# Filter rows by part in natural column order, in a spectral-mixing and MLP kernel on one core

## The chip, the cores and the metric

The kernel runs on one core of a Trainium2 chip. The metric is the device time of one execution in microseconds (us), median of several executions. A run's state is called fast when it is undisturbed; all timed comparisons below use fast runs. The engines are named as in the profile: PE is TensorE's matmul, PEld its weight load, DVE is VectorE, ACT is ScalarE, POOL is GpSimd, SP is SyncE, which issues most DMA transfers. TensorE's results go to PSUM, in this kernel in banks of 512 fp32 per partition; the other operands lie in SBUF, and an "eviction" is the copy from PSUM to SBUF. The "stationary" operand of a matmul is the one that the weight load brings in. The "tail" is what follows the last computed output.

## The reference

A sequence of 2048 positions with 512 features goes through two residual blocks. The first multiplies its two-dimensional real Fourier transform by a complex filter; the second is an MLP over the sequence axis.

```python
def _A_ref(x, w_r, w_i):                 # x: 1 x 2048 x 512, w: 2048 x 257
    X = jnp.fft.rfft2(x.astype(jnp.float32), axes=(-2, -1))
    X = X * (w_r + 1j * w_i)
    return jnp.fft.irfft2(X, s=(S, D), axes=(-2, -1)).astype(jnp.bfloat16)

h  = x + _A_ref(_layernorm(x), A_w_r, A_w_i)
h2 = h + _B_ref(_layernorm(h), B_w1, B_b1, B_w2, B_b2)   # MLP over S, 1376 hidden, gelu
```

## The kernel before

All transforms are matrix products. The parts that matter here:

- "Transform 2" turns Y into half spectra along the features. Even and odd columns of the spectrum need different sums, so it has two parities `par`. Its eviction goes to CS.
- "Mixing" (X) combines the rows of CS in two half-height matmuls, so that each of 128 partitions holds a component of one row. Partition order is given by `_row`.
- The "filter multiply" V = PSUM x W on VectorE multiplies the mixed values by the real and by the imaginary part of the filter (index `w` or "part").
- "G1" uses slices of V as the stationary operand of the first inverse step.

CS and V are kept parity by parity: first the 128 odd columns, then the 128 even ones. The filter lies in memory in natural column order, so VectorE reads it with a step of two.

```python
def _row(sign, comp, k2, s):
    return 4 * (k2 * 2 + s) + 2 * sign + comp
...
add("CS", [NP, 16, 2, 2, NP], bf, rd)     # group, parity, component, column
add("W", [NP, NG, 2, LW], bf, rw)         # filter: row group, part, 257 columns
add("V", [NP, NG, 2, 256], bf, rv)
...
# filter loads: rows of 514 bytes, 28 transfers in all
for comp in range(2):
    d = W[comp::4, g0:g0 + ng, w, :]
    dma(..., d, bass.AP(dram.tensor, g0 * LW, [[64 * LW, 32], [LW, ng], [1, LW]]), ...)
    d = W[2 + comp::4, h0:h0 + nh, w, :]  # mirrored rows, in descending order
    dma(..., d, bass.AP(dram.tensor, (64 - h0) * LW, [[64 * LW, 32], [-LW, nh], [1, LW]]), ...)
...
# transform 2: four matmuls fill one PSUM bank of 512 fp32, then one eviction
mm(f"f2_{G}_{par}{b}", lambda bank, par=par: ps[:, bank, par * 256:par * 256 + 256],
   Y[:, b, par, 2 * G:2 * G + 2, :]..., E[:, b, par, :], unit, b == 0, b == 1, ...)
dst = CS[:, G, :, :, :].rearrange("p y c j -> p (y c j)")
cs_ops[G] = act(f"cs_{G}", dst, lambda bank: ps[:, bank, :], ACT.Copy, 512, unit=unit, prio=14)
...
# mixing, then the filter multiply on VectorE
mm(f"x_{G}_{c}{r}", ..., M[rows, ..., c, :], CS[rows, G, :, c, :], ...)
win = bass.AP(wt.tensor, wt.offset + 1, [list(wt.ap[0]), [LW, 2 * ng], [1, 2], [2, NP]])
eng.tensor_tensor(vout, s, win, ALU.mult)   # s: fp32 in PSUM, each row used for both parts
...
# G1
mm(f"g1_{g}_{par}{w}", ..., V[:, g, w, par * NP:par * NP + NP], R[:, 1 if g == 0 else 0, w, :], ...)
```

A list scheduler in the kernel fixes the order of each engine's instructions when the program is built.

Of the kernel before, what the change touches and what calls it, by code (L numbers as in the profile page):

```python
# [9 lines left out]
NP = 128  # L10
# [3 lines left out]
NG = 32  # L14
F_LEN = 1376
NFT = 11
LW = 257
# [17 lines left out]


def _row(sign, comp, k2, s):
    return 4 * (k2 * 2 + s) + 2 * sign + comp


def _fwd_matrices(special):
# [381 lines left out]
def memory_layout():  # L423
    L = []
    bf = dt.bfloat16
    f32 = dt.float32
    cur = [0]

    def region(nbytes):
        o = cur[0]  # L430
        cur[0] += (nbytes + 31) // 32 * 32
        return o

    def add(name, shape, dty, off):
        L.append((name, shape, dty, off))
        return off

    add("X", [NP, NS2, D_LEN], bf, region(16384))
    rb = region(16384)
    add("PQ", [NP, 2, 2, NS2, NP], bf, rb)  # L440
    add("GT", [NP, NFT, D_LEN], bf, rb)
    rc = region(16384)
    add("Y", [NP, 2, 2, NG, 64], bf, rc)
    add("EO", [NP, NS2, D_LEN], bf, rc)
    add("OUT", [NP, NS2, D_LEN], bf, rc)
    rd = region(16384)
    add("CS", [NP, 16, 2, 2, NP], bf, rd)
    add("H", [NP, NS2, D_LEN], bf, rd)
    rw = region(2 * NG * LW * 2)
    add("W", [NP, NG, 2, LW], bf, rw)  # L450
    add("HH", [NP, NS2, D_LEN], bf, rw)
    rv = region(32768)
    add("V", [NP, NG, 2, 256], bf, rv)
    add("W1", [NP, NS2, F_LEN], bf, region(NS2 * F_LEN * 2))
    for t in range(NFT):
        add(f"W2_{t}", [NP, S_LEN], bf, rv + t * 4096 if t < 8 else rw + 16384 + (t - 8) * 4096)
    add("FP", [NP, NS2, 2, NP], bf, region(8192))
    add("FS", [NP, NS2, 2, NP], bf, rv)
    add("EM", [NP, 3072], bf, region(6144))
    add("IF", [NP, NS2, NP], bf, region(4096))  # L460
    for i in range(3):
        add(f"TT{i}", [NP, 2, 256], f32, region(2048))
    for i in range(4):
        add(f"JK{i}", [NP, D_LEN], bf, region(1024))
    add("st", [NP, NS2, 8], f32, region(512))
    add("mv", [NP, NS2, 2], f32, region(128))
    for nm in ("sm", "nm", "v1", "rs", "v2", "r2"):
        add(nm, [NP, NS2], f32, region(64))
    add("eps", [NP, 8], f32, region(32))
    add("ZT", [NP, D_LEN], bf, region(1024))  # L470
    add("bv", [NP, NS2], f32, region(64))
    add("tb", [NP, 8], f32, region(32))
    add("B1s", [NP, 16], bf, region(32))
    add("B1f", [NP, 16], f32, region(64))
    add("B2s", [NP, NS2], bf, region(32))
    add("B2f", [NP, NS2], f32, region(64))
    return L
# [13 lines left out]
def build_kernel(nc, A_x, A_w_r, A_w_i, B_w1, B_b1, B_w2, B_b2, out):  # L491
# [29 lines left out]
    def mm(name, outf, lhsT, rhs, unit, start, stop, first, prio, n, ins=None, half=False, after=()):  # L521
        occ = n / 2.4 + 3.0
        if half:
            occ = occ / 2
        if n == 128:
            occ = 61.0
        return K.op(name, "pe", lambda eng, bank: eng.matmul(outf(bank), lhsT, rhs, start=start, stop=stop),  # L527
                    ins=ins or [lhsT, rhs], occ=occ, lat=n / 2.4 + 220.0, unit=unit, pw=True, first=first, prio=prio, after=after)
# [46 lines left out]
    for ch, (u0, u1) in enumerate(((0, 1), (1, 4), (4, 8))):  # L575
        g0, ng = 4 * u0, 4 * (u1 - u0)
        lst = []
        for w, dram in ((0, A_w_r), (1, A_w_i)):
            for comp in range(2):
                d = W[comp::4, g0:g0 + ng, w, :]  # L580
                lst.append(dma(f"ld_wp{ch}_{w}{comp}", d, bass.AP(dram.tensor, g0 * LW, [[64 * LW, 32], [LW, ng], [1, LW]]),
                               32 * ng * 514, prio=42 - ch, group=f"w{ch}", rate=300.0))
                h0, nh = (g0, ng) if g0 else (1, ng - 1)
                d = W[2 + comp::4, h0:h0 + nh, w, :]
                lst.append(dma(f"ld_wm{ch}_{w}{comp}", d, bass.AP(dram.tensor, (64 - h0) * LW, [[64 * LW, 32], [-LW, nh], [1, LW]]),
                               32 * nh * 514, prio=42 - ch, group=f"w{ch}", rate=300.0))
                if g0 == 0:
                    d = W[2 + comp::4, 0, w, :]
                    lst.append(dma(f"ld_wz{ch}_{w}{comp}", d, bass.AP(dram.tensor, 32 * LW, [[64 * LW, 32], [1, LW]]),
                                   32 * 514, prio=42 - ch, group=f"w{ch}", rate=300.0))  # L590
        for u in range(u0, u1):
            wload[u] = lst
    dma("ld_D2", EM[:, 2048:3072], cin["EM"][:, 2048:3072], 1 << 18, outs=[EM[:, 2048:3072]], prio=30)
# [72 lines left out]
    for q in range(8):  # L666
        for b in range(2):
            unit = PsumUnit("f1", 1)
# [28 lines left out]
    def stage_f2(u):  # L697
        for i in range(2):
            G = 2 * u + i
            unit = PsumUnit("f2", 1)  # L700
            for par in range(2):
                for b in range(2):
                    mm(f"f2_{G}_{par}{b}", lambda bank, par=par: ps[:, bank, par * 256:par * 256 + 256],
                       Y[:, b, par, 2 * G:2 * G + 2, :].rearrange("p g k -> p (g k)"), E[:, b, par, :],
                       unit, b == 0, b == 1, par == 0 and b == 0, 10, 256)
            dst = CS[:, G, :, :, :].rearrange("p y c j -> p (y c j)")
            if G == 1:
                cs_ops[G] = dve(f"cs_{G}", lambda eng, bank, dst=dst: eng.tensor_copy(dst, ps[:, bank, :]), [], [dst], 512, unit=unit, prio=14)
            else:
                cs_ops[G] = act(f"cs_{G}", dst, lambda bank: ps[:, bank, :], ACT.Copy, 512, unit=unit, prio=14)  # L710

    def stage_x(u):
        unit = PsumUnit("x", 2)
        first = True
        grp = [cs_ops[2 * u + 1]]
        for i in range(2):
            G = 2 * u + i
            for c in range(2):
                for r in range(2):
                    rows = slice(64 * r, 64 * r + 64)  # L720
                    mm(f"x_{G}_{c}{r}", lambda bank, r=r, i=i: ps[:, bank + r, i * 256:i * 256 + 256],
                       M[rows, 1 if G == 0 and r == 0 else 0, c, :], CS[rows, G, :, c, :], unit, c == 0, c == 1, first, 13, 256, half=True, after=grp)
                    first, grp = False, ()
        g0 = 4 * u
        nh = 2 if u in V_SPLIT else 1
        ng = 4 // nh
        for h in range(nh):
            wt = W[:, g0 + h * ng:g0 + h * ng + ng, :, :]
            win = bass.AP(wt.tensor, wt.offset + 1, [list(wt.ap[0]), [LW, 2 * ng], [1, 2], [2, NP]])
            vout = V[:, g0 + h * ng:g0 + h * ng + ng, :, :].rearrange("p g w l -> p (g w l)")  # L730

            def tt(eng, bank, h=h, win=win, vout=vout):
                s = psf[:, bank * 512 + h * 512:bank * 512 + h * 512 + 256 * ng]
                s = bass.AP(s.tensor, s.offset, [list(s.ap[0]), [256, ng], [0, 2], [1, 256]])
                return eng.tensor_tensor(vout, s, win, ALU.mult)  # L735
            K.op(f"v_{u}_{h}", "dve", tt, ins=[wt], outs=[vout], occ=50.0 + 2130.0 / nh, lat=170.0 + 2130.0 / nh, unit=unit, pr=True,
                 last=h == nh - 1, prio=11, after=wload[u])
# [3 lines left out]
    def stage_g1(u):  # L741
        for h in range(2):
            nw = G1_WARM.get((u, h), 0)
            unit = PsumUnit("g1", 1, early=nw > 0)
            for w_ in range(nw):
                warm(f"warmg{u}{h}{w_}", unit, 10, first=w_ == 0, after=[lastg1[0]])
            for gi in range(2):
                g = 4 * u + 2 * h + gi
                for par in range(2):
                    for w in range(2):  # L750
                        lastg1[0] = mm(f"g1_{g}_{par}{w}", lambda bank, gi=gi, par=par: ps[:, bank, gi * 256 + par * 128:gi * 256 + par * 128 + 128],
                           V[:, g, w, par * NP:par * NP + NP], R[:, 1 if g == 0 else 0, w, :], unit, w == 0, w == 1,
                           gi == 0 and par == 0 and w == 0 and not nw, 12, 128)
            g0 = 4 * u + 2 * h
            dst = PQ[:, :, :, :, 4 * g0:4 * g0 + 8].rearrange("p y q n (g k) -> p (y q n) g k", k=4)

            def src(bank):
                return ps[:, bank, :].rearrange("p (g m k) -> p m g k", g=2, k=4)
            act(f"pq_{u}_{h}", dst, src, ACT.Copy, 512, unit=unit, prio=15)
# [117 lines left out]
```

## Time and profile before

| What | Before |
|---|---|
| time, median of 3 runs | 134.35 us (134.19 to 134.53) |
| span of the profiled execution | 133.0 us |
| first V multiply starts, last one ends | 22.0, 39.9 us |
| V multiplies | 17.9 us, no gap |
| spacing of transform-2 matmuls | 0.109 us |

The chain of waits goes back from the last instruction to what released it. Columns: start in us, length in us, what.

```profile
17.63 1.47 ACT Y L545 x3
...
19.15 2.77 PE ps L527 x25
...
22.02 1.04 DVE V L735
...
23.16 15.62 DVE V L735 x8
...
38.91 0.62 PE ps L527 x8
```

So from 22 to 39.9 us VectorE decides, and TensorE matters only if it makes VectorE wait. The groups by shape tell what one instruction of this part costs. Columns: line, engine, operation, output and inputs, shapes, count; busy time and mean ns of one; idle time before, with what ended it.

```profile
L527 PEld LDWEIGHTS ps<-GT,W 128*128 128x128 bf16 x160 | 23.1, 144 | 11.5
...
L735 DVE TENSOR_TENSOR V<-ps,W 128x2048 bf16<-128x2048 f32 x6 | 13.3, 2282 | 0.0
...
L527 PE MATMUL ps<-EM,Y 128*128 128x256 bf16 x64 | 8.7, 273 | 0.4 <-ACT Y L545 0.4
...
L527 PEld LDWEIGHTS ps<-EM,V 128*128 128x128 bf16 x128 | 7.5, 98 | 2.3 <-issue 1.4 <-DVE V L735 0.8
```

The mean of a matmul (273 ns in transform 2) is its latency; what it takes from TensorE is the spacing of starts (0.109 us), which the timeline shows (start, length of the whole group, operation, count):

```profile
25.21 1.91 PE L527 MATMUL ps<-EM,Y 128*128 128x256 bf16 x16
27.06 0.61 PE L527 MATMUL ps<-CS,EM 64*128 64x256 bf16 x8
27.60 0.45 PE L527 MATMUL ps<-EM,V 128*128 128x128 bf16 x5
```

Within the first group the spacing is (1.91 - 0.273) / 15 = 0.109 us.

The windows view gives busy times in a stretch (PE, PEld, DVE, ACT, POOL), then granted clock, DMA share and GB/s. While the filter arrives (16 to 30 us) the DMA engines are full at 280 GB/s; with the MLP's first weights, in rows of 11 KB (40 to 45 us), they reach 428.

```profile
16.00:30.00 14.00, 13.48 (x155) 9.91 (x153) 11.66 (x14) 10.70 (x23) 1.81 (x8) 1.00 1.03 280
40.00:45.00 5.00, 4.31 (x40) 3.47 (x40) 1.83 (x5) 3.61 (x8) 0.00 (x0) 1.00 1.02 428
```

### The profile page before, as it was taken

To read this page: it belongs to the slowest core of one execution; us is meant where nothing else is said; L and a number is where in the kernel's file an instruction comes from. 1 tells how busy PE (TensorE), PEld (TensorE's weight loads), DVE (VectorE), ACT (ScalarE), POOL (GpSimd) and SP (SyncE) were. 2 spreads that over 40 slices of the span, in tenths; PEclk is the share of its full clock that TensorE was granted. 3 is DMA by queue.
4 is the path that set the end of the run, shared out by engine and by line. 5 is a ranking of instruction groups with operands and counts; after the bars stand their busy time and mean duration, and the time that the engine had idled before them with its cause. 6 is when DMAs were issued, how large, how long until landed. Compare 5 with 4: busy or idle time off the path is not lost.

```text
span 133.0 us, 2023 instructions
## 1 busy us (share of the span) xinstructions
PE 125.4 (94%) x786; PEld 75.3 (57%) x786; DVE 69.2 (52%) x127; ACT 63.4 (48%) x146; POOL 12.2 (9%) x33
## 2 busy tenths in 40 slices
PE   6999989999987979999999999999999999999990
PEld 2356756878656726644434444456666666666660
DVE  0379975999990999999970000000242332423322
ACT  4569976878966999986679322222000000000000
POOL 0288830000300000000000000000000000000000
PEclk9999999999999999999999999999999999999999
DMA  3999698999999999992000000000111112111121
GB/s 94 335 370 382 178 276 229 304 317 264 411 430 430 398 411 409 419 281 89 0 0 0 0 0 0 5 0 0 39 39 64 55 39 81 42 59 59 39 79 39
DMA packets 16648, 22.16 MB, mean 167 GB/s; under 512 B 2720, under 2 KB 12960, under 8 KB 16128
## 3 DMA queue, kind: packets, MB, share of 16 engines
q1 hardware_dynamic: 16352, 21.52, 47.3%
q10 hardware_dynamic: 288, 0.52, 1.3%
q8 instruction: 6, 0.10, 0.3%
q14 instruction: 2, 0.02, 0.0%
HBM read 19.95 MB, written 2.10 MB: 166 GB/s over the span
## 4 chain that ended last, share of the span: by engine, by line
PE 51%; DVE 33%; ACT 8%; DMA 5%; issue 1%; SPq 1%; DVEq 0%; ACTq 0%
PE ps L527 50%; DVE V L735 13%; DVE H L795 7%; DMA X<-in_A_x_dram 5%; ACT Y L545 5%; DVE TT L786 4%; DVE TT L788 4%; DVE HH L800 4%; ACT rs L545 1%; ACT FS L545 1%; DVE st L649 1%; SPq L517 1%; DVE OUT L825 1%; ACT PQ L545 0%; PE ps L617 0%
## 5 line engine op out<-in xcount | busy, mean ns | idle before, releaser
L527 PE MATMUL ps<-HH,W 128*128 128x512 bf16 (+1 forms) x176 | 40.7, 379 | 1.2 <-DVE HH L800 0.9
L527 PE MATMUL ps<-GT,W 128*128 128x512 bf16 (+1 forms) x176 | 38.2, 379 | 0.0
L825 DVE SCALAR_TENSOR_TENSOR OUT<-ps,B2f,H 128x512 bf16<-128x512 f32 x16 | 12.0, 750 | 48.7 <-PE ps L527 48.7
L527 PEld LDWEIGHTS ps<-GT,W 128*128 128x128 bf16 (+1 forms) x176 | 25.4, 144 | 12.7
L527 PEld LDWEIGHTS ps<-HH,W 128*128 128x128 bf16 (+1 forms) x176 | 17.2, 100 | 21.2 <-DVE HH L800 1.9
L735 DVE TENSOR_TENSOR V<-ps,W 128x2048 bf16<-128x2048 f32 (+1 forms) x10 | 17.9, 1856 | 0.9 <-PE ps L527 0.9
L545 ACT ACTIVATE GT<-ps,B1f 128x512 bf16<-128x512 f32 (+1 forms) x11 | 7.1, 688 | 14.6 <-PE ps L527 14.6
L545 ACT ACTIVATE JK<-H,nm 128x512 bf16<-128x512 bf16 x16 | 11.6, 724 | 3.0 <-DVE H L795 2.9
L617 PE MATMUL ps<-ZT 128*128 128x512 bf16 x34 | 11.3, 479 | 1.3 <-DVE ZT L613 1.2
L649 DVE BATCH_NORM_STATS2 st<-X 128x6 f32<-128x512 bf16 x14 | 9.3, 668 | 5.3 <-DMA X<-in_A_x_dram 5.3
L795 DVE TENSOR_TENSOR H<-ps,TT 128x512 bf16<-128x512 f32 x16 | 10.9, 681 | 0.0
L545 ACT ACTIVATE PQ<-ps 128x512 bf16<-128x512 f32 x16 | 8.9, 603 | 3.5 <-PE ps L527 3.2
L545 ACT ACTIVATE EO<-ps 128x512 bf16<-128x512 f32 x16 | 9.3, 599 | 0.9 <-PE ps L527 0.9
L527 PE MATMUL ps<-EM,V 128*128 128x128 bf16 x128 | 9.2, 219 | 0.5 <-DVE V L735 0.5
L527 PE MATMUL ps<-EM,PQ 128*128 128x256 bf16 x64 | 9.0, 273 | 0.7 <-ACT PQ L545 0.7
L545 ACT ACTIVATE CS<-ps 128x512 bf16<-128x512 f32 x15 | 8.3, 608 | 2.1 <-PE ps L527 2.1
L527 PE MATMUL ps<-EM,Y 128*128 128x256 bf16 x64 | 8.7, 273 | 0.4 <-ACT Y L545 0.4
L527 PEld LDWEIGHTS ps<-EM,V 128*128 128x128 bf16 x128 | 7.5, 98 | 2.3 <-issue 1.4
L629 POOL TENSOR_SCALAR FS<-FP,rs 128x256 bf16<-128x256 bf16 x9 | 8.3, 935 | 1.3 <-ACT rs L545 1.3
L527 PE MATMUL ps<-FS,X 128*128 128x256 bf16 x64 | 8.3, 273 | 0.1
L786 DVE TENSOR_TENSOR TT<-ps,X 128x256 f32<-128x256 f32 x16 | 6.7, 416 | 3.3 <-PE ps L527 3.3
L527 PEld LDWEIGHTS ps<-EM,PQ 128*128 128x128 bf16 x64 | 6.2, 98 | 2.9 <-ACT PQ L545 0.9
(36 smaller groups left out, 80.3 us busy)
## 6 DMA issues: line engine op xcount, KB each, us to landing
W<-in_B_w_dram SPq DMA_DIRECT2D x4, 1376.0 KB, 11.0
W<-in_B_w_dram SPq DMA_DIRECT2D x10, 512.0 KB, 17.6
out_dram<-OUT SPq DMA_DIRECT2D x16, 128.0 KB, 1.7
W<-in_A_w_r_dram SPq DMA_DIRECT2D x4, 257.0 KB, 4.3
W<-in_A_w_i_dram SPq DMA_DIRECT2D x4, 257.0 KB, 5.0
X<-in_A_x_dram SPq DMA_DIRECT2D x4, 256.0 KB, 5.8
X<-in_A_x_dram SPq DMA_DIRECT2D x2, 512.0 KB, 7.7
W<-in_A_w_r_dram SPq DMA_DIRECT2D x4, 192.8 KB, 3.5
```

What stands on the lines that cost most here:

```text
L517: return eng.dma_start(dst, src)
L527: return K.op(name, "pe", lambda eng, bank: eng.matmul(outf(bank), lhsT, rhs, start=start, stop=stop), ins=ins or [lhsT, rhs], occ=occ, la ...
L545: return eng.activation(dst, s, func, **kw)
L617: return K.op(name, "pe", lambda eng, bank: eng.matmul(ps[:, bank, :], ZT[:, 0:NP], ZT[:, :], start=True, stop=True), ins=[ZT[:, :]], occ= ...
L629: dve(f"fs{i}", lambda eng, bank: eng.tensor_scalar(FS[:, i, :, :], FP[:, i, :, :], rs, None, op0=ALU.mult), [FP[:, i, :, :], rs], [FS[:, ...
L649: dve(f"st_{i}", lambda eng, bank, i=i, x=x: eng.bn_stats(ST[:, i, 0:6], x), [x], [ST[:, i, 0:6]], 512, prio=25)
L735: return eng.tensor_tensor(vout, s, win, ALU.mult)
L786: dve(f"tl_{s2}", lambda eng, bank, tt=tt, xl=xl: eng.tensor_tensor(tt[:, 0, :], ps[:, bank, 256:512], xl, ALU.add), [xl], [tt[:, 0, :]], ...
L788: dve(f"th_{s2}", lambda eng, bank, tt=tt, xh=xh: eng.tensor_tensor(tt[:, 1, :], xh, ps[:, bank, 256:512], ALU.subtract), [xh], [tt[:, 1, ...
L795: return eng.tensor_tensor(hs.rearrange("p (h d) -> p h d", h=2), e, tt[:, :, :], ALU.add)
L800: dve(f"hh_{s2}", lambda eng, bank, s2=s2, hs=hs: eng.tensor_scalar(HH[:, s2, :], hs, NM[:, s2:s2 + 1], R2[:, s2:s2 + 1], op0=ALU.add, op1 ...
L825: dve(f"fin{s2}", lambda eng, bank, dst=dst, bia=bia, hs=hs: eng.scalar_tensor_tensor(dst, ps[:, bank, :], bia, hs, op0=ALU.add, op1=ALU.add),
```

## The change

The filter is kept part by part (real, then imaginary), rows next to each other. With a new partition order, the un-mirrored rows of both components come in one transfer whose rows are as long as the chunk (2 to 8 KB), and 28 filter transfers become 20. VectorE then reads the filter contiguously, in natural column order. CS and V must be in that order too. TensorE makes it: transform 2 writes each parity into every second fp32 of the PSUM bank, and G1 picks a parity by loading every second column of V.

```diff
-    return 4 * (k2 * 2 + s) + 2 * sign + comp
+    return 4 * (k2 * 2 + s) + 2 * comp + sign
...
-    add("CS", [NP, 16, 2, 2, NP], bf, rd)
+    add("CS", [NP, 16, 2, 256], bf, rd)
-    add("W", [NP, NG, 2, LW], bf, rw)
+    add("W", [NP, 2, NG, LW], bf, rw)
...
+            d = W[0:NP:2, w, g0:g0 + ng, :].rearrange("p g l -> p (g l)")
+            lst.append(dma(f"ld_wp{ch}_{w}", d, bass.AP(dram.tensor, g0 * LW, [[64 * LW, 32], [0, 2], [1, ng * LW]]), ...))
             for comp in range(2):
-                d = W[comp::4, g0:g0 + ng, w, :]
-                lst.append(dma(f"ld_wp{ch}_{w}{comp}", d, bass.AP(dram.tensor, g0 * LW, [[64 * LW, 32], [LW, ng], [1, LW]]), ...))
-                d = W[2 + comp::4, h0:h0 + nh, w, :]
+                d = W[1 + 2 * comp::4, w, h0:h0 + nh, :]
...
-                    mm(f"f2_{G}_{par}{b}", lambda bank, par=par: ps[:, bank, par * 256:par * 256 + 256],
+                    mm(f"f2_{G}_{par}{b}", lambda bank, par=par: ps[:, bank, :].rearrange("p (c j y) -> p y c j", c=2, y=2)[:, par, :, :],
...
-                       M[rows, 1 if G == 0 and r == 0 else 0, c, :], CS[rows, G, :, c, :], ...
+                       M[rows, 1 if G == 0 and r == 0 else 0, c, :], CS[rows, G, c, :], ...
...
-            win = bass.AP(wt.tensor, wt.offset + 1, [list(wt.ap[0]), [LW, 2 * ng], [1, 2], [2, NP]])
+            win = bass.AP(wt.tensor, wt.offset + 1, [list(wt.ap[0]), [LW, ng], [NG * LW, 2], [1, 256]])
...
-                           V[:, g, w, par * NP:par * NP + NP], R[:, 1 if g == 0 else 0, w, :], ...
+                           V[:, g, w, par::2], R[:, 1 if g == 0 else 0, w, :], ...
```

## The prediction

> **What bounds the kernel now.** The chain of waits (133.0 us profile) has four parts. Until 19.1 us: loads of x, statistics and forward transform 1 (ACT's Y evictions at the end). Then transform 2 ("F2", matmuls ps<-EM,Y) and the first mixing matmuls ("X", ps<-CS,EM) up to 22.0. From 22.0 to about 39.9 VectorE multiplies by the filter (V<-ps,W): ten instructions without a gap, 17.9 us. After that VectorE again (43 to 68) and TensorE alone (68.6 to 129.7). The change touches only the second and third part.

> **What the change removes.** Half of the 514-byte filter rows arrive as long rows, 28 filter transfers become 20. In the windows view the DMA engines are saturated from 16 to 30 us at only 250 to 320 GB/s, but reach over 400 once the large weights load (35 to 50 us). So about 2.1 of the 4.2 MB should go from about 270 to 400 GB/s: an estimate of 2.5 us less DMA time, plus 8 x 0.62 us less issuing on SyncE. But by the list of waits no V multiply and no matmul waits for a filter or weight load; the first V waits 0.9 us, for TensorE. Worth on the critical path: about 0.

> **What it does not gain.** V takes 2.282 us for 2048 and 1.217 us for 1024 elements: 1.04 ns an element[...], with step-2 filter reads. Contiguous reads can't improve that: the PSUM operand stays fp32, and the final addition, fp32 PSUM with contiguous bf16, runs no faster (750 ns for 512). V stays at 2.28 us.

> **What it adds.** (a) F2 writes PSUM with a step of 2 fp32 (8 bytes). [...] No trace of this case shows it yet: all matmul outputs before are contiguous. [...]I estimate double spacing: F2 now runs at 109 ns (16 in 1.91 us), so 216 ns, 64 x 0.107 = +6.9 us of TensorE. (b) The last step ("G1", ps<-EM,V) loads weights with a step of 2 bf16. Weights with step 16 (GT,W) take 144 ns against 98 contiguous; [...]I expect 98 to 105 ns and a G1 spacing still about 56 ns.

> **How much is critical.** From 19.15 to 40.6 TensorE needs 64 x 0.109 + 64 x 0.054 + 128 x 0.056 = 17.6 us of 21.5. It has little slack under VectorE. Walking through the order of its groups with F2 at 216 ns: the first V starts about 1.5 us later (17 F2 precede the first X), and V stalls three more times, 0.7 to 1.3 us each, when a block of F2 precedes its X. Last V ends about 45.1 instead of 39.9: +5. Nothing later absorbs it. Earlier filters give nothing back.

> **Prediction.** 138.8 us, range 134.0 to 141.0. Chances: faster by over 2% 0.03, within 2% 0.29, slower 0.68.

> **What would show it.** Right: F2's spacing near 216 ns (or matmul durations above 273 ns), first V near 23.5 us, VectorE gaps waiting for TensorE between V's, V still 2.28 us each, filter transfers landing earlier without effect, times after the last V unchanged but shifted. Wrong: F2 still at 109 ns spacing; then about 134.3.

> **What would make it wrong.** Strided PSUM writes may be free (unchanged time, the main alternative) or cost much more than double (over 141). Step-2 weight loads may slow G1 (128 loads, up to 0.046 us each, +3 us more). A changed order of instructions, as the schedule depends on modelled transfer times, could move things by a microsecond. A gain over 2% would need V to be faster per element, which I think excluded.

No term of the sum goes with them: +6.9 us of TensorE time in transform 2, of which the walk through the groups puts 5.2 on the last V (45.1 against 39.9); 134.35 + 5.2 = 139.55 us, forecast as 138.8. The double spacing in (a) is the author's estimate from the measured 109 ns; at that time nothing showed the factor (e1 below measured it). So is the 98 to 105 ns in (b), from the measured 98 and 144 ns, and the 0.054 us of a mixing matmul, half of 0.109.

## The result

The changed kernel takes 140.91 us (140.88 to 141.27, 4 runs) against 134.40 us (4 runs); the ratio is 1.0492, 95% interval 1.047 to 1.0514. Ratios here and below are the mean time of one kernel's fast runs over that of the other's of the same rounds, so not quite the ratio of the medians quoted. The instructions of TensorE, VectorE and ScalarE stand in the same order in both kernels; only the transfers and some small GpSimd work moved.

The chain of waits after:

```profile
17.52 1.47 ACT Y L545 x3
18.99 0.05 issue
19.03 22.51 PE ps L527 x198
...
41.57 3.43 DVE V L735 x2
...
45.14 0.62 PE ps L527 x8
```

Where VectorE's multiplies stood in the chain, 198 matmuls now stand in one unbroken piece. VectorE is no longer the limit of this stage; TensorE is. The groups by shape:

```profile
L527 PE MATMUL ps<-EM,Y 128*128 128x256 bf16 x64 | 15.3, 416 | 0.4 <-ACT Y L545 0.4
L735 DVE TENSOR_TENSOR V<-ps,W 128x2048 bf16<-128x2048 f32 x6 | 13.6, 2286 | 4.5 <-PE ps L527 4.5
...
L527 PEld LDWEIGHTS ps<-EM,V 128*128 128x128 bf16 x128 | 7.9, 100 | 2.5 <-issue 1.4 <-DVE V L735 0.6
...
L527 PEld LDWEIGHTS ps<-EM,Y 128*128 128x128 bf16 x64 | 7.6, 127 | 5.0 <-ACT Y L545 0.7 <-issue 0.6 <-DVE Y L688 0.3
```

Transform-2 matmuls rose from 273 to 416 ns. The weight loads of G1, now with a step of two, stayed at 98 to 100 ns. The V multiply with contiguous filter reads stayed at 2.28 us. VectorE idled 4.5 us before V multiplies of the large shape (and 1.9 before the first small one), each time for TensorE. On the timeline of VectorE (the time in brackets is its idle time before):

```profile
23.56 6.75 DVE L735 TENSOR_TENSOR V<-ps,W 128x1024 bf16<-128x1024 f32 x4 [1.90 <-PE ps L527]
32.16 4.49 DVE L735 TENSOR_TENSOR V<-ps,W 128x2048 bf16<-128x2048 f32 x2 [1.85 <-PE ps L527]
37.84 2.29 DVE L735 TENSOR_TENSOR V<-ps,W 128x2048 bf16<-128x2048 f32 x1 [1.20 <-PE ps L527]
41.57 4.55 DVE L735 TENSOR_TENSOR V<-ps,W 128x2048 bf16<-128x2048 f32 x3 [1.43 <-PE ps L527]
```

The V stage starts 1.54 us later (23.56 against 22.02) and has three gaps of 1.85, 1.20 and 1.43 us. It ends at 46.1 instead of 39.9. The last output of the kernel is computed 6.22 us later (135.98 against 129.76), so nothing after the stage gave any of it back. The same stretch of TensorE's timeline:

```profile
27.93 3.62 PE L527 MATMUL ps<-EM,Y 128*128 128x256 bf16 x16
31.48 0.61 PE L527 MATMUL ps<-CS,EM 64*128 64x256 bf16 x8
32.02 0.45 PE L527 MATMUL ps<-EM,V 128*128 128x128 bf16 x5
```

The spacing is (3.62 - 0.42) / 15 = 0.213 us, and the group holds TensorE 3.55 us instead of 1.85.

The transfers did what was intended. The last filter load was issued by 19.2 us instead of 25.9, and the first MLP weights at 27.0 instead of 30.5. In the 16 to 30 us window the rate rose from 280 to 310 GB/s. This window understates the gain, since after 19.2 us other loads are issued in it; from 10 to 19 us, when mostly filter rows are in flight, the windows view shows 277 GB/s before and 366 after.

```profile
16.00:30.00 14.00, 13.52 (x100) 8.26 (x98) 9.88 (x13) 8.38 (x18) 0.62 (x2) 1.00 1.02 310
```

### The profile page after: what moved, and what is told of

Its sections match the earlier page's. It is cut to its first block, busy times and chain, and to the rows that moved or that the text cites. A ratio compares the mean times of both kernels' runs of the same rounds, so it can differ in the third digit from the quotient of the medians.

```text
span 138.9 us, 2005 instructions
## 1 busy us (share of the span) xinstructions
PE 131.2 (94%) x776; PEld 77.5 (56%) x786; DVE 69.4 (50%) x127; ACT 64.3 (46%) x146; POOL 12.2 (9%) x33
## 4 chain that ended last, share of the span: by engine, by line
PE 62%; DVE 22%; ACT 7%; DMA 4%; issue 1%; SPq 1%
PE ps L527 62%; DVE H L795 7%; ACT Y L545 5%; DMA X<-in_A_x_dram 4%; DVE TT L786 4%; DVE TT L788 4%; DVE HH L800 4%; DVE V L735 2%; ACT rs L545 1%; ACT FS L545 1%; DVE st L649 1%; SPq L517 1%; DVE OUT L825 1%; ACT PQ L545 0%; PE ps L617 0%
## 5 line engine op out<-in xcount | busy, mean ns | idle before, releaser
L527 PE MATMUL ps<-EM,Y 128*128 128x256 bf16 x64 | 15.3, 416 | 0.4 <-ACT Y L545 0.4
L545 ACT ACTIVATE CS<-ps 128x512 bf16<-128x512 f32 x15 | 8.9, 597 | 6.7 <-PE ps L527 6.5
L527 PEld LDWEIGHTS ps<-EM,Y 128*128 128x128 bf16 x64 | 7.6, 127 | 5.0 <-ACT Y L545 0.7
```

The lines of the kernel that those rows point to most:

```text
L527: return K.op(name, "pe", lambda eng, bank: eng.matmul(outf(bank), lhsT, rhs, start=start, stop=stop), ins=ins or [lhsT, rhs], occ=occ, la ...
L545: return eng.activation(dst, s, func, **kw)
```

## The experiments

Theory A: the whole loss is TensorE time in transform 2, caused by PSUM writes that are not contiguous. Rival B: step-2 weight loads, or the new filter layout and its transfers, cost it. All kernels below gave the right result.

### e1: strided PSUM writes alone

The kernel before; only the output of transform 2 is interleaved, and the eviction reads it back in parity order.

```diff
-   lambda bank, par=par: ps[:, bank, par * 256:par * 256 + 256]
+   lambda bank, par=par: ps[:, bank, :].rearrange("p (n y) -> p y n", y=2)[:, par, :]
    # eviction: dst "p y (c j)"
-   lambda bank: ps[:, bank, :]
+   lambda bank: ps[:, bank, :].rearrange("p (n y) -> p y n", y=2)
```

> The kernel before with one edit: transform 2 writes PSUM with a step of two fp32, and the eviction reads it back so that everything after it is as before (filter layout, transfers, contiguous weights of the last mixing step). Theory A (strided PSUM writes slow TensorE): matmuls ps<-EM,Y spaced 0.22 us instead of 0.109, the first V multiply near 23.5 us, about 140 to 141 us. Theory B (the cost of the change lies in step-2 weight loads or in the new filter transfers): 134.4 us.

Measured: 140.80 us, ratio 1.0475 (1.046 to 1.0491). Nearly the whole loss is there, without new transfers, filter layout or strided weights. From the view of tile Y (duration min/median/max in ns, first and last start):

```profile
L527 PEld LDWEIGHTS ps<-EM,Y x64: 95/139/139, 19.1 to 41.5; 128*128 128x128 bf16 x64
L527 PE MATMUL ps<-EM,Y x64: 379/421/421, 19.1 to 41.7; 128*128 128x256 bf16 x64
```

The ScalarE evictions, which now read PSUM with a step of two, still took 597 ns (median). The weight loads of these matmuls show 139 instead of 98 ns, although they load the same contiguous data; the matmuls beside them went from 273 to 421 ns.

### e2: the change with contiguous PSUM writes

The changed kernel; transform 2 writes as before, and the eviction interleaves while it reads.

```diff
-   lambda bank, par=par: ps[:, bank, :].rearrange("p (c j y) -> p y c j", c=2, y=2)[:, par, :, :]
+   lambda bank, par=par: ps[:, bank, par * 256:par * 256 + 256]
-   lambda bank: ps[:, bank, :]                                       # eviction
+   lambda bank: ps[:, bank, :].rearrange("p (y c j) -> p c j y", y=2, c=2)
```

> The changed kernel with one edit: transform 2 writes PSUM contiguously again and the eviction on ScalarE (one on VectorE) does the interleaving while it reads PSUM. Long-row transfers, natural column order, contiguous filter reads and step-2 weights all stay. Theory A: back to 134.2 to 134.8 us, V multiplies without gaps, evictions still 0.60 us. Theory B: stays at 139 to 141 us. If reading PSUM at alternating places slows the eviction, CS evictions are longer than 0.60 us and the time lies between.

Measured: 134.64 us, ratio 1.0014 (0.9999 to 1.0029). The loss is gone, while long rows, natural order, contiguous filter reads and step-2 weights are all still there. Together with e1, B falls. The V stage on VectorE's timeline is again one piece:

```profile
21.94 17.88 DVE L735 TENSOR_TENSOR V<-ps,W 128x1024 bf16<-128x1024 f32 x10 [0.94 <-PE ps L527]
```

The interleaving eviction costs nothing: ScalarE's median is 599 ns against 597. From the view of tile CS, e2 and then the kernel before:

```profile
L545 ACT ACTIVATE CS<-ps x15: 591/599/641, 20.0 to 35.6; 128x512 bf16<-128x512 f32 x15
```

```profile
L545 ACT ACTIVATE CS<-ps x15: 592/597/645, 20.1 to 35.6; 128x512 bf16<-128x512 f32 x15
```

### e3, e4 and e9: which writes are slow

Three patterns on the kernel before, each undone by the eviction: runs of two fp32 on 8-byte boundaries with a gap of two (e3); single fp32 with a step of four (e4); runs of two, shifted by one fp32 for one parity, and the left-over places for the other (e9). "Theory A1" is the guess that aligned pairs of fp32 run at full speed, and that a lone fp32 costs the same at every step.

```diff
-   lambda bank, par=par: ps[:, bank, par * 256:par * 256 + 256]
+   e3: ps[:, bank, :].rearrange("p (n y i) -> p y n i", y=2, i=2)[:, par, :, :]
+   e4: ps[:, bank, par * 256:par * 256 + 256].rearrange("p (n k) -> p k n", k=4)
+   e9: bass.AP(v.tensor, v.offset + (1, 0)[par], [list(v.ap[0]), [4, 128], [(1, 3)[par], 2]])   # v = ps[:, bank, :]
```

> The kernel before with transform 2 writing PSUM in runs of two fp32 (8 bytes, aligned) with a gap of two; the eviction undoes it. Theory A1 [...]: full speed, spacing 0.109 us, 134.4 us. Theory A2 (any interruption of the contiguous write costs): spacing 0.2 us or more, about 140 us.

> The kernel before with transform 2 writing PSUM with a step of four fp32 (16 bytes) within its own 256 columns; the eviction undoes it. Theory A1 [...]: the same as step two, spacing 0.22 us, 140 to 141 us. Theory A3 (the cost grows with the step): spacing well over 0.22 us, 145 us or more.

> As the run with runs of two fp32, but shifted by one fp32: the even half writes contiguous runs of two that start 4 bytes off an 8-byte boundary, the odd half writes the places left over (first and fourth of every four). The evictions are two halves each, so the total time is no measure; the matmul durations are. If PSUM takes two columns at once only when both lie in one aligned 8 bytes: all 64 matmuls ps<-EM,Y take about 421 ns. If any run of two is enough: 32 of them take about 273 ns and 32 about 421 (or the odd half is fast too).

Measured: e3 134.53 us, ratio 1.0002 (0.9986 to 1.0019): full speed. e4 140.69 us, ratio 1.0468 (1.0448 to 1.0488): a larger step is no worse than two. e9 was one look without rounds (140.45 us, state unknown, not comparable as a time, since its evictions are split); its durations decide. The tile view of e3, then of e9:

```profile
L527 PE MATMUL ps<-EM,Y x64: 272/273/283, 19.2 to 35.6; 128*128 128x256 bf16 x64
```

```profile
L527 PE MATMUL ps<-EM,Y x64: 379/421/421, 19.1 to 41.6; 128*128 128x256 bf16 x64
```

### e5: the same extra TensorE time without strides

The kernel before; the first matmul of each accumulation is issued three times and the first two results are thrown away, so that transform 2 has twice the matmuls in the same order.

```diff
-   eng.matmul(outf(bank), lhsT, rhs, start=start, stop=stop)
+   [eng.matmul(outf(bank), lhsT, rhs, start=start, stop=stop or i < rep - 1) for i in range(rep)][-1]   # rep = 3 where b == 0
```

> The kernel before with every second matmul of transform 2 issued three times (the first two results are thrown away), so the stage has 128 contiguous matmuls instead of 64 in the same order; nothing is strided. If the loss of the change is only the extra TensorE time of this stage: 64 x 0.109 = 7.0 us more TensorE work, the same gaps between V multiplies (about 1.9, 1.9, 1.2, 1.4 us) and 140 to 141 us. If strided writing also costs elsewhere (slower reading of PSUM, a blocked bank), the loss is visibly smaller here than 6.3 us.

Measured: 140.97 us, ratio 1.0477 (1.0461 to 1.0493), the same as e1. The gaps on VectorE's timeline are nearly those of the change:

```profile
23.95 6.75 DVE L735 TENSOR_TENSOR V<-ps,W 128x1024 bf16<-128x1024 f32 x4 [2.02 <-PE ps L527]
32.51 4.49 DVE L735 TENSOR_TENSOR V<-ps,W 128x2048 bf16<-128x2048 f32 x2 [1.81 <-PE ps L527]
38.33 2.29 DVE L735 TENSOR_TENSOR V<-ps,W 128x2048 bf16<-128x2048 f32 x1 [1.33 <-PE ps L527]
41.96 4.55 DVE L735 TENSOR_TENSOR V<-ps,W 128x2048 bf16<-128x2048 f32 x3 [1.34 <-PE ps L527]
```

Strided writing costs TensorE time and nothing else that these runs show.

### e6: natural order with short rows

The kernel of e2 with the filter loaded in 28 transfers of 512-byte rows (columns 1 to 256 alone).

```diff
-    add("W", [NP, 2, NG, LW], bf, rw)
+    add("W", [NP, NG, 2, 256], bf, rw)
-            d = W[0:NP:2, w, g0:g0 + ng, :].rearrange("p g l -> p (g l)")      # one transfer, long rows
+                d = W[comp::4, g0:g0 + ng, w, :]     # source offset + 1, [[64 * LW, 32], [LW, ng], [1, 256]]
```

> The eviction-interleave kernel (natural column order, contiguous PSUM writes) with the filter loaded in short rows again: 28 transfers of 512-byte rows, columns 1 to 256 alone, parts together. Compared with the run that interleaves in the eviction, it takes the long rows alone away. If the filter loads are off the critical path: 134.2 to 134.7 us, filter transfers ending about 5 us later, large weight loads starting about 30.5 us instead of 27. If long rows gain or cost something hidden: a difference of over 0.4 us from the eviction-interleave run.

Measured: 134.41 us, ratio 0.9995 (0.9983 to 1.0008). The MLP's weights are issued at 29.8 us again instead of 26.8 in e2, and the time does not care: the gain of the long rows is real (270 GB/s in e6 against 316 in e2 from 0 to 19 us), but off the critical path. The windows view of e6 and then of e2, 16 to 30 us:

```profile
16.00:30.00 14.00, 13.48 (x155) 9.90 (x153) 11.66 (x14) 10.70 (x23) 1.79 (x8) 1.00 1.01 285
```

```profile
16.00:30.00 14.00, 13.52 (x155) 9.93 (x154) 11.54 (x14) 10.71 (x23) 0.86 (x3) 1.00 1.04 315
```

In this stretch, with rows of 512 bytes (e6), the DMA engines moved 285 GB/s at a share of 1.01, and with rows of 514 bytes (the kernel before) 280 at 1.03; with rows of 11 KB, from 40 to 45 us of the kernel before, 428 at 1.02. The 512-byte rows start 514 bytes apart in memory; aligned ones were not tried.

Long rows alone, without natural order, stay untried.

### e7 and e8: using the contiguous filter

The natural order makes the filter contiguous for VectorE, but the other operand is fp32 in PSUM, and nothing was gained (2.286 against 2.282 us). That VectorE would be about twice as fast with every operand contiguous and in 16 bits was the guess. To test it, e7 lets ScalarE first copy the mixed values to SBUF as bf16, for groups 2 and 4 of eight, and e8 for groups 2, 4 and 6. The base is e6.

```diff
+            if u in X_ACT:
+                act(f"xs_{u}", xs[:, :], lambda bank: psf[:, bank * 512:bank * 512 + 1024], ACT.Copy, 1024, unit=unit, ...)
+                eng.tensor_tensor(vout, xin, win, ALU.mult)      # xin: xs, each row used for both parts
```

> As the short-row natural-order kernel, but for two of the eight filter groups (2 and 4) ScalarE first copies the mixed values from PSUM to SBUF as bf16, so that VectorE multiplies bf16 by bf16, all contiguous. If contiguous 16-bit operands double VectorE's rate: those two multiplies take about 1.2 us instead of 2.28 us, V stage 15.7 us instead of 17.9, and about 132.5 us if TensorE and ScalarE keep up; 134.4 if one of them becomes the limit. If not: 2.28 us and 134.4 us or more.

> The same with three of the eight groups (2, 4 and 6). VectorE's part falls by about 3.2 us, ScalarE's rises by 3 us, and TensorE needs about 18.6 us of the stage: I expect TensorE or ScalarE to become the limit, 132 to 133.5 us, not much better than with two.

Measured: e7 134.98 us, ratio 1.003 (1.0018 to 1.0043); e8 134.33 us, ratio 0.9987 (0.9975 to 1.0). I missed both times: e8 was expected at 132 to 133.5 us, e7 at 132.5, or at 134.4 if TensorE or ScalarE became the limit, and it is above even that. The packing works, as the groups of e7 show:

```profile
L746 DVE TENSOR_TENSOR V<-ps,W 128x2048 bf16<-128x2048 f32 x4 | 9.1, 2286 | 2.6 <-PE ps L531 2.6
...
L739 DVE TENSOR_TENSOR V<-XS,W 128x2048 bf16<-128x2048 bf16 x2 | 2.4, 1214 | 0.0
L549 ACT ACTIVATE XS<-ps 128x1024 bf16<-128x1024 f32 x2 | 2.1, 1045 | 0.0
```

A multiply takes 1.214 instead of 2.286 us, 1.88 times as fast, but VectorE then waits for TensorE: 2.6 us before the large multiplies. The longest of these waits, 2.24 us, ends at 32.23; from 30.28 to 31.17 TensorE runs 16 matmuls of G1, ahead of the mixing group that VectorE needed. So a part of the wait, some 0.9 us, is the order on TensorE. That the order took the whole gain away is my reading and not shown; the next runs test it in part.

### e10, e11 and e12: the order mended

Groups 3 and 6 are packed, and the priorities of the scheduler retuned (transform 2 above G1, its evictions first; e11 also shares PSUM units differently). e12 is the control with e10's priorities for transform 2, its evictions and G1, but no packing. The settings were picked with the kernel's own scheduling model.

```diff
-X_ACT = ()
+X_ACT = (3, 6)                                   # e10, e11
     transform 2 matmul prio 10 -> 12 (e10, e12), 13 (e11);  eviction of CS 14 -> 16;  G1 12 -> 11
-    K = Builder(nc, {"f1": 6, "f2": 2, "x": 2, "g1": 2, ...
+    K = Builder(nc, {"f1": 6, "f2": 3, "x": 1, "g1": 3, ...                        # e11 only
```

> The packed multiply for groups 3 and 6, with the priorities of the kernel's scheduler retuned (transform 2 above the last mixing step, evictions of transform 2 first). VectorE's stage falls from 17.9 to about 15.8 us; the last V multiply should end about 1.5 us earlier than the 39.9 us of before. If TensorE keeps up: about 132.9 us, ratio 0.988 to 0.992. If TensorE is the limit again, as with groups 2 and 4: 134 us or more.

> The same two groups, with PSUM shared out otherwise as well (three transform-2 units and one mixing unit of two banks open at a time, in place of two and two). By the modelled order 0.2 us better than the run with priorities alone, 132.7 us; one open mixing unit may instead make VectorE wait for TensorE at each multiply that reads PSUM, 133.5 us or more.

> The control for the two packed runs: the same new priorities, no packed multiply. VectorE needs its 17.9 us whatever TensorE's order is: 134.2 to 134.8 us. A time near 133 would mean that the new order and not the packed multiply gives the gain.

Measured: e10 133.31 us, ratio 0.9913 (0.9899 to 0.9926). e11 133.22 us, ratio 0.9906 (0.9891 to 0.9921). e12 134.35 us, ratio 0.9993 (0.9981 to 1.0006). The new order alone gives nothing; with the packing it gives 0.9%. That is below the 2% that counts as a change, but clear of the noise, and it beats both kernels. e10 and e11 can't be told apart; both were 0.4 to 0.5 us above the 132.9 and 132.7 us that were expected. What the retuning itself is worth stays open: e7 and e10 differ both in the groups packed (2 and 4, 3 and 6) and in the priorities, and no run packs 3 and 6 with the old priorities, or 2 and 4 with the new. The control, e12, on VectorE's timeline:

```profile
21.93 17.81 DVE L746 TENSOR_TENSOR V<-ps,W 128x1024 bf16<-128x1024 f32 x10 [0.93 <-PE ps L531]
```

The V stage of e11 on VectorE's timeline ends at 38.2 us instead of 39.9:

```profile
21.96 6.75 DVE L746 TENSOR_TENSOR V<-ps,W 128x1024 bf16<-128x1024 f32 x4 [0.94 <-PE ps L531]
28.82 1.23 DVE L739 TENSOR_TENSOR V<-XS,W 128x2048 bf16<-128x2048 bf16 x1
29.97 4.48 DVE L746 TENSOR_TENSOR V<-ps,W 128x2048 bf16<-128x2048 f32 x2
34.72 1.23 DVE L739 TENSOR_TENSOR V<-XS,W 128x2048 bf16<-128x2048 bf16 x1 [0.27 <-ACT XS L549]
35.86 2.35 DVE L746 TENSOR_TENSOR V<-ps,W 128x1024 bf16<-128x1024 f32 x2
```

## Why the prediction was right or wrong

- **What bounds the stage, and transfers worth nothing: right.** No V multiply and no matmul waited for a filter load before or after; e6 against e2 shows both row lengths at the same time within 0.2%.
- **V stays at 2.28 us: right** (2.286). The step of the filter does not matter beside an fp32 operand in PSUM: 2.282 us with step two, 2.286 contiguous. With bf16 on both sides the same multiply takes 1.214 us (e7), so it is the other operand that holds it. Whether its type or its place does is not separated, since e7 changed both.
- **Step-2 weight loads free: right.** 98 to 100 ns and G1 spaced 0.056 us; e2 has them at 98 ns and loses nothing, and e1 shows 100 ns with contiguous loads. The step of 16 (GT,W) takes 144 ns. Why the one costs time and the other none was not shown.
- **Strided PSUM writes double transform 2: right.** Forecast 0.216 us, measured 0.213. First V forecast near 23.5 us, measured 23.56. Three more gaps were forecast, and three came.
- **How much of it is critical: the step that failed. One term of TensorE's time was too small.** The walk through the groups gave a last V at 45.1 us, +5.2; it ended at 46.1, +6.2. The gaps were forecast as 0.7 to 1.3 us and measured 1.85, 1.20 and 1.43. The faulty term is the one written "64 x 0.054": I took half of a transform-2 matmul for a mixing matmul that uses half of the array's rows, so 0.43 us for each group of eight. A group holds TensorE 0.54 us until the next group starts, before and after alike; at its inner spacing, (0.61 - 0.269) / 7 = 0.049 us, eight would make 0.39. The group in front of it, too, holds TensorE about 0.1 us longer than its spacing says (1.85 against 16 x 0.109, 3.55 against 16 x 0.213 = 3.41). In front of G1, which uses all rows like transform 2, there is no such excess: six matmuls of transform 2 hold it 0.66 us, which is 6 x 0.109.

```profile
22.90 0.83 PE L527 MATMUL ps<-EM,Y 128*128 128x256 bf16 x6
23.56 0.61 PE L527 MATMUL ps<-EM,V 128*128 128x128 bf16 x8
```

  So the sum left out the time around each switch to half-height matmuls and back: 0.54 us instead of 0.43 for the group, and about 0.1 us more for the group in front of it. In the changed kernel TensorE was held 22.40 us from 19.03 until the mixing group before the last gap ends at 41.43. The prediction's own terms for these matmuls, 62 x 0.216 + 56 x 0.054 + 80 x 0.056, make 20.90. Of the missing 1.5 us, 0.77 lie in the seven mixing groups (3.79 against 3.02), 0.38 in transform 2 and 0.36 in G1. The walk missed 1.0 of them. This account is worked out from the timeline; no experiment changed the number of switches. All these starts stood in the profile before. With them TensorE had less slack than "17.6 of 21.5 us" says.
- **The point was lower than its own argument.** 134.35 + 5.2 is 139.55; I gave 138.8, pulled towards the 0.29 chance that strided writes are free. The measured 140.91 lies at the very edge of the range, which had too little room above. Of the 2.1 us from 138.8 to 140.91, 0.75 is this, 1.0 the walk, and about 0.3 the rest below.
- **A small rest is open.** Last output to last output the kernels differ by 6.22 us, the times by 6.5. Time outside the profiled span is 1.5 us before and in e1, but 1.9 to 2.0 us in all runs of the change and of e2, which share the long-row transfers; within the span their tail is 0.3 us shorter. What this comes from was not tested.

## What to carry to other kernels

Keep TensorE's PSUM output contiguous, or at least in aligned pairs of fp32 (273 ns a matmul in e3, as when contiguous), and let the eviction do any reordering: in these runs ScalarE reordered while reading PSUM at no cost (597 to 599 ns against 597), whereas TensorE paid a factor of 1.95 (0.213 against 0.109 us). An engine that is off the chain of waits is only free as far as its slack goes; reckon the slack from the starts of whole groups, which include the switches between full-height and half-height matmuls (here 0.54 us for eight half-height ones, not 0.39), and not from the spacing inside a group. When a rewrite makes an operand contiguous, ask whether the other operand lets the engine use it: here the faster multiply (1.214 against 2.286 us) came with both in 16 bits in SBUF, and a gain in time only where TensorE kept up.
